# Two evacuation edits in an attention and two-layer feed-forward kernel on one core: who copies the first layer's sums, and where the second layer's stores stand

## The chip, the core and the metric

One Trainium2 chip, of which one core is used. Its engines each work through their own queue in order: PE (TensorE) multiplies and writes into PSUM, ACT (ScalarE) and DVE (VectorE) read PSUM and do element-wise work, SP (SyncE) issues all the DMA transfers of this kernel. The metric is the device time of one execution in microseconds (us); the time before is the median of three runs.

## The reference

Attention in chunks, then two feed-forward layers over the 3072 tokens of 512 features (`B*S` by `H*D`), all in float32:

```
out = _attn_ref(q, k, v, mem_k, mem_v)      # chunks of 32 queries, 64 keys each: 8 memory + 16 left + 32 + 8 right
x   = out.transpose(0, 2, 1, 3).reshape(B * S, H * D)
h   = np.maximum(x @ w_in, 0.0)             # layer 1: 512 -> 2048
x   = h * h @ w_out                         #          2048 -> 512
h   = x @ w_in2                             # layer 2: 512 -> 2048
g   = np.maximum(h, 0.0) + np.log1p(np.exp(-np.abs(h)))
y   = g @ w_out2                            #          2048 -> 512
```

## The kernel before

**Numbers.** Each float32 operand is split into a high and a low half; a product is three matmuls of 128x128 by 128x512 (high by low, low by high, high by high). ACT makes the high half (a cast) and DVE the low half (a subtraction).

**Layer 1** runs over six blocks of 512 tokens, n = 0 to 5, and in each over 16 steps f = 0 to 15. A step is written in `step(n, f)`: 12 matmuls into a PSUM buffer `hp` (`h_mm`, L292 to L294), then on ACT the relu, the square and the high half `gh` (`act1`, L304, L305, L307, through the buffer `r`), on DVE the low half `gl` (`act1_low`, L313), which is written down one step later, and 12 matmuls that add into the four PSUM accumulators `acc` of the block (`out_mm`, L328). These 12 lag by two steps (`LOOK = 2`), so that the last one of block n is issued behind the `hp` matmuls of step 0 of block n+1, and the first one of block n+1 behind those of its step 2. Between the steps stand the attention of the next block (scores L156, softmax on DVE and ACT L176 to L188, the transposes of the probabilities on DVE L202 in two batches of eight, the values L237) and the preparation of layer 2's weights (loads `cf<-w` L379, then L384 on ACT and L388 to L392 on DVE, split and stored). In all this part the order of every engine is the written one (`manual_schedule()`).

When the sums of a block are complete, `evac` (L333) copies the four accumulators to SBUF, two on ACT (L339) and two on DVE (L337) in turn, and stores each to DRAM (L340). The SBUF tile comes from `tmp`, a tag with three buffers, which the relu's `r` uses as well. A buffer that is handed out again waits until its last reader is done; for `ev` that is the store.

The attention's result of the next block is gathered in the tile `xf` (`p_out`, L253, tag `xf`, one buffer), written at steps 3, 7, 11 and 14, and read at step 15 by `x_split` (L267, L268), which makes layer 1's operands. In the last block `x_load` (L486) uses the same tag for layer 2's input.

**Layer 2** runs over three groups of two blocks. `first_stage` has eight chunks p of 42 matmuls (36 in the first) into PSUM banks (`product`, L745), in which seven products replace eight; ACT copies partial sums to `h` (L775, L777, L784, L765), DVE adds (L786, L792, L794), and `softplus` (L751 to L757: three operations on ACT, four on DVE, in the buffers `cf`) follows. `second_stage` has 16 steps f of 24 matmuls (L833) into all eight PSUM banks, and `g_split` (L404, L399) makes the halves for it. When the 16 steps are done, the eight banks are copied, four on ACT into `cf` (L843) and four on DVE into `tmp` (L840), and stored (L845). Weights are reloaded by `fetch` (L375) in six places, one load as a place comes free; the last `fetch` of a group stands at f = 15. In layer 2 only PE's order is the written one. That of ACT, DVE and SP is set by the scheduler that compiles the kernel, from its own estimate of when things are ready.

Of the kernel before, what the change touches and what calls it, by code (L numbers as in the profile page):

```python
# [10 lines left out]
F32 = mybir.dt.float32  # L11
# [9 lines left out]
P = 128  # L21
# [7 lines left out]
KD = DM // P  # L29
KF = DFF // P  # L30
# [3 lines left out]
BLK = 512  # L34
# [8 lines left out]
NCF = 3  # L43
# [12 lines left out]
def body(ctx: ExitStack, tc: tile.TileContext, qk, vW, w1, w2, out):  # L56
    nc = tc.nc
# [3 lines left out]
    xpool = ctx.enter_context(tc.tile_pool(name="xpool", bufs=1))  # L61
# [6 lines left out]
    x2s = [dram.tile([P, KD, BLK], F32, name=f"x2s{i}") for i in range(NB)]  # L68
# [12 lines left out]
    def cf_tile(k=None, shape=(P, 2, DM), dtype=F32):  # L81
        if k is None:
            k = cf_at[0] = (cf_at[0] + 1) % NCF
        return sb.tile(list(shape), dtype, tag=f"cf{k}", name="cf", bufs=1)
# [230 lines left out]
    acc = [None] * 4  # L315
# [15 lines left out]
                )  # L331

    def evac(blk):  # L333
        for m in range(4):
            e = tmp("ev")
            if m % 2:
                nc.vector.tensor_copy(e, acc[m])  # L337
            else:
                nc.scalar.copy(out=e, in_=acc[m])  # L339
            nc.sync.dma_start(out=x2s[blk][:, m, :], in_=e)  # L340


    at_ctx = tc.tile_pool(name="at", bufs=1)
# [5 lines left out]
    def tmp(name):  # L349
        return sb.tile([P, BLK], F32, tag="tmp", name=name, bufs=3)  # L350
# [11 lines left out]
    def out_step():  # L362
        n, f, g, cols = pending.pop(0)
        out_mm(f, g, cols)
        if f == KF - 1:
            evac(n)
# [119 lines left out]
    def x_load(grp, k):  # L486
        t = xpool.tile([P, 2, 2, BLK], F32, tag="xf", name="x2f")
        for i in range(2):
            nc.sync.dma_start(out=t[:, :, i], in_=x2s[2 * grp + i][:, k::2])
        xf_t[2, grp, k] = t  # L490

    def x_jobs(grp, k):
        d = {}

        def sums(i):
            b11, b12, b21, b22 = (xf_t[2, grp, k][:, j // 2, j % 2] for j in range(4))
            if i == 0:
                if grp == 0:
                    t = late[0].tile([P, 4, BLK], F32, tag="r2", name="xs")
                    d["t"] = t[:, 0], t[:, 1], t[:, 2]  # L500
                else:
                    d["t"] = [tmp("xs") for _ in range(3)]
            t3, t2, t4 = d["t"]
            if i == 0:
                todo = (t3, b22, b12), (b12, b12, b11)
            else:
                todo = (t2, b22, b12), (t4, b21, t2)
            for o, a, b in todo:
                nc.vector.tensor_tensor(out=o, in0=a, in1=b, op=ALU.subtract)
            d["x"] = b11, b12, t2, b22, b21, t3, t4  # L510

        def split(i):
            if k == 0:
                xo[grp, i] = wpool.tile([P, 2, 2, BLK], F32R, tag=f"w{i}", name=f"xo{i}")
            t = xo[grp, i]
            halves(t[:, 0, k], t[:, 1, k], d["x"][i], late=(grp == 0))

        return [lambda: sums(0), lambda: sums(1)] + [lambda i=i: split(i) for i in range(7)]


    with tc.manual_schedule(engines={mybir.EngineType.SP}):
# [198 lines left out]
        def fetch():  # L720
            i = at_load[0]
            if i == len(loads):
                return
            at_load[0] += 1
            key, src = loads[i]
            pool, tag = places[i % len(places)]
            t = pool[0].tile(list(src.shape), F32R, tag=tag, name="ws")
            store(t, src)
            ws[key] = t

        def bank():
            i = at_bank[0] = (at_bank[0] + 1) % 8
            if i < 4:
                return (ps, pl[0])[i % 2].tile([P, BLK], F32, tag="ps", name="bk")
            return pa.tile([P, DM], F32, tag=f"acc{i - 4}", name="bk")
# [12 lines left out]
        def softplus(p, i):  # L748
            h = ht[p][:, i]
            z, l, c = (cf_tile(k) for k in range(3))  # L750
            nc.scalar.activation(out=z, in_=h, func=AF.Abs)  # L751
            nc.scalar.activation(out=z, in_=z, func=AF.Exp, scale=-1.0)
            nc.scalar.activation(out=l, in_=z, func=AF.Ln, bias=1.0)
            nc.vector.tensor_scalar(out=c, in0=z, scalar1=1.0, scalar2=-1.0, op0=ALU.add, op1=ALU.add)
            nc.vector.tensor_tensor(out=c, in0=z, in1=c, op=ALU.subtract)  # L755
            nc.vector.scalar_tensor_tensor(out=h, in0=h, scalar=0.0, in1=l, op0=ALU.max, op1=ALU.add)
            nc.vector.tensor_tensor(out=h, in0=h, in1=c, op=ALU.add)  # L757

        def g_split(f, t):
            g = gs[f, t] = g_tiles()  # L760
            halves(*g, ht[f // 2][:, f % 2, t])

        def last_product(grp, p, a):
            product(grp, 6, ws.pop((grp, "b", p))[:, 1], a, False)
            nc.scalar.copy(out=ht[p][:, 1, 0], in_=a)  # L765
            fetch()
# [35 lines left out]
        def second_stage(grp, prev):  # L802
            banks = {}
            if grp + 1 < NGR:
                todo = {f: [] for f in range(KF)}
                for k in range(2):
                    j = x_jobs(grp + 1, k)
                    for f, n in zip((3, 4, 5, 6, 7) if k == 0 else (9, 10, 11, 12, 13), (2, 2, 2, 2, 1)):
                        todo[f] += j[:n]
                        j = j[n:]  # L810
            for f in range(KF):
                w = ws[grp, "o", f // 2][:, f % 2]
                if grp + 1 < NGR and f in (1, 8):
                    x_load(grp + 1, f // 8)
                if f + 1 < KF:
                    for t in range(2):
                        g_split(f + 1, t)
                for i in SOFT_B.get(f, ()):
                    softplus(i // 2, i % 2)
                if grp + 1 < NGR:  # L820
                    for job in todo[f]:
                        job()
                for t in range(2):
                    gh, gl = gs.pop((f, t))
                    for m in range(4):
                        if f == 0:
                            banks[t, m] = bank()
                            if (t, m) == (0, 3):
                                last_product(grp, *prev)
                        bk = banks[t, m]  # L830
                        s = slice(m * P, (m + 1) * P)
                        for j, (a, b) in enumerate(((gh[:, s], w[:, 1]), (gh[:, s], w[:, 0]), (gl[:, s], w[:, 0]))):
                            nc.tensor.matmul(out=bk, lhsT=a, rhs=b, start=(f == 0 and j == 0), stop=(f == KF - 1 and j == 2))  # L833
                if f % 2:
                    fetch()
            for t in range(2):
                for m in range(4):
                    if m % 2:
                        e = tmp("ev")
                        nc.vector.tensor_copy(e, banks[t, m])  # L840
                    else:
                        e = cf_tile((2 * t + m // 2) % NCF)[:, 0]
                        nc.scalar.copy(out=e, in_=banks[t, m])  # L843
                    r = (2 * grp + t) * BLK + m * P
                    nc.sync.dma_start(out=out[r:r + P, :], in_=e)  # L845

        xq = {}
        for k in range(2):
# [17 lines left out]
        with tc.manual_schedule(engines={mybir.EngineType.PE}):  # L866
            for grp in range(NGR):
                second_stage(grp, first_stage(grp))
# [45 lines left out]
```

## Time and profile before

| | us |
|---|---|
| median of 3 runs (1121.87 to 1123.51) | 1122.61 |
| the profiled execution | 1124.83 |
| its span in the trace | 1123.1 |
| PE busy | 1088.1 (97%) |
| DVE busy | 761.0 (68%) |
| ACT busy | 589.8 (53%) |
| mean granted TensorE clock | 0.988 of full speed |

Rows of a timeline read: start in us from the span's start, duration, engine, line, operation, output from inputs, shapes, count, and in brackets the idle time of that engine just before, with what ended it. "<-DVE gl L313" means that the wait was ended by DVE's instruction of line 313 that wrote `gl`. A matmul row lasts longer than the distance to the next one, since matmuls overlap; the distance is what counts.

### The profile page before, as it was taken

The numbers are of one execution on the slowest core, as the hardware profiler recorded it, in microseconds if no ns is written. First come the engines' busy times: TensorE is split into PE (matmuls) and PEld (weight loads), VectorE is DVE, ScalarE is ACT, GpSimd is POOL, SyncE is SP. The second block draws the span as 40 slices with busy tenths as digits, with TensorE's granted clock in tenths as the row PEclk, the third lists the DMA queues.
The fourth block names the chain that finished last, engine by engine and source line by source line (L and its number), as shares of the span: only waits on it lengthen the run. The fifth ranks groups of instructions, "written<-read, shape, count | busy, mean of one in ns | idle before, by whom it ended". The sixth has DMA issues, their size and how long they took to land.

```text
span 1123.1 us, 18576 instructions
## 1 busy us (share of the span) xinstructions
PE 1088.1 (97%) x7592; PEld 893.1 (80%) x7592; DVE 761.0 (68%) x1239; ACT 589.8 (53%) x914; POOL 0.7 (0%) x6
## 2 busy tenths in 40 slices
PE   5899999999999999999999999999999999999998
PEld 4668878878887887788888878888788888788887
DVE  6899576667667666785533499953598963699822
ACT  3567544444554445454544577642577642676622
POOL 0000000000000000000000000000000000000000
PEclk9899999999999999999999999999999999999999
DMA  9941244445335544343440755422655441755202
GB/s 365 379 186 54 63 138 144 147 156 175 102 118 173 175 147 164 132 168 132 149 142 1 265 192 208 170 103 103 207 197 215 150 141 66 244 191 221 76 1 75
DMA packets 49428, 174.99 MB, mean 156 GB/s; under 512 B 5312, under 2 KB 5312, under 8 KB 41152
## 3 DMA queue, kind: packets, MB, share of 16 engines
q1 hardware_dynamic: 49344, 173.82, 44.2%
q8 instruction: 59, 0.97, 0.3%
q14 instruction: 25, 0.20, 0.1%
HBM read 138.15 MB, written 35.65 MB: 155 GB/s over the span
## 4 chain that ended last, share of the span: by engine, by line
PE 88%; DVE 6%; DMA 2%; ACT 2%; issue 1%; SPq 0%; DVEq 0%; ACTq 0%
PE bk L833 23%; PE acc L328 22%; PE bk L745 18%; PE hp L292 7%; PE hp L293 7%; PE hp L294 7%; PE xs L237 1%; DMA out<-cf 1%; DVE pt L202 1%; PE xs L156 1%; DMA x2s<-ev 1%; DVE cf L110 1%; DVE cf L107 1%; PE sc L156 1%; PE xp L237 1%
## 5 line engine op out<-in xcount | busy, mean ns | idle before, releaser
L328 PE MATMUL acc<-gh,w 128*128 128x512 f32 (+1 forms) x776 | 243.1, 395 | 0.9 <-DVE w L122 0.9
L833 PE MATMUL bk<-ws,gh 128*128 128x512 f32 x768 | 236.5, 389 | 0.0
L745 PE MATMUL bk<-xo,ws 128*128 128x512 f32 x1008 | 230.8, 390 | 2.3 <-ACT h L784 1.5
L745 PEld LDWEIGHTS bk<-xo,ws 128*128 128x128 f32 x1008 | 188.9, 188 | 43.0 <-ACT h L784 2.3
L328 PEld LDWEIGHTS acc<-gh,w 128*128 128x128 f32 x776 | 146.8, 191 | 31.8 <-DVE w L122 1.3
L833 PEld LDWEIGHTS bk<-ws,gh 128*128 128x128 f32 x768 | 144.1, 188 | 30.2
L328 PE MATMUL acc<-gl,w 128*128 128x512 f32 (+1 forms) x388 | 153.5, 396 | 11.7 <-DVE gl L313 11.7
L292 PE MATMUL hp<-xh,w 128*128 128x512 f32 (+1 forms) x388 | 154.8, 399 | 3.5 <-ACT pt L218 3.1
L293 PE MATMUL hp<-xl,w 128*128 128x512 f32 (+1 forms) x388 | 152.7, 393 | 0.0
L294 PE MATMUL hp<-xh,w 128*128 128x512 f32 (+1 forms) x388 | 152.0, 392 | 0.0
L833 PE MATMUL bk<-ws,gl 128*128 128x512 f32 x384 | 149.4, 389 | 0.0
L399 DVE TENSOR_TENSOR gl<-h,gh 128x512 fp32r<-128x512 f32 x96 | 66.1, 690 | 84.3 <-ACT gh L404 84.0
L404 ACT CAST gh<-h 128x512 fp32r<-128x512 f32 x96 | 59.4, 622 | 112.2 <-PE bk L833 111.9
L304 ACT ACTIVATE r<-hp 128x512 f32<-128x512 f32 (+1 forms) x97 | 57.2, 590 | 110.5 <-PE hp L294 96.6
L313 DVE TENSOR_TENSOR gl<-r,gh 128x512 fp32r<-128x512 f32 (+1 forms) x97 | 66.3, 683 | 67.2 <-ACT gh L307 66.7
L328 PEld LDWEIGHTS acc<-gl,w 128*128 128x128 f32 x388 | 74.2, 191 | 29.8 <-DVE gl L313 14.5
L292 PEld LDWEIGHTS hp<-xh,w 128*128 128x128 f32 x388 | 74.6, 192 | 19.8 <-ACT pt L218 3.3
L294 PEld LDWEIGHTS hp<-xh,w 128*128 128x128 f32 x388 | 74.7, 193 | 15.4
L293 PEld LDWEIGHTS hp<-xl,w 128*128 128x128 f32 x388 | 74.6, 192 | 14.7 <-DVE xl L282 0.2
L833 PEld LDWEIGHTS bk<-ws,gl 128*128 128x128 f32 x384 | 72.1, 188 | 14.7
L202 DVE STREAM_TRANSPOSE pt<-t 32x128 f32<-32x128 f32 x256 | 77.5, 303 | 4.3
L751 ACT ACTIVATE cf<-h 128x1024 f32<-128x1024 f32 x48 | 51.0, 1062 | 27.8 <-DVE cf L755 19.9
(82 smaller groups left out, 1143.6 us busy)
## 6 DMA issues: line engine op xcount, KB each, us to landing
ws<-wa SPq DMA_DIRECT2D x24, 1024.0 KB, 4.9
ws<-wo SPq DMA_DIRECT2D x24, 1024.0 KB, 4.8
ws<-wb SPq DMA_DIRECT2D x24, 768.0 KB, 4.4
r<-w SPq DMA_DIRECT2D x16, 1024.0 KB, 10.6
cf<-w SPq DMA_DIRECT2D x32, 512.0 KB, 5.1
qk<-qk SPq DMA_DIRECT2D x46, 336.0 KB, 4.9
v<-vW SPq DMA_DIRECT2D x44, 256.0 KB, 4.9
wo<-cf SPq DMA_DIRECT2D x16, 512.0 KB, 2.9
```

What stands on the lines that cost most here:

```text
L202: nc.vector.transpose(pt[b:b + 32, g], t[g * 32:(g + 1) * 32, i, h])
L292: nc.tensor.matmul(out=hp, lhsT=b, rhs=xh[:, c], start=(c == 0), stop=False)
L293: nc.tensor.matmul(out=hp, lhsT=a, rhs=xl[:, c], start=False, stop=False)
L294: nc.tensor.matmul(out=hp, lhsT=a, rhs=xh[:, c], start=False, stop=(c == KD - 1))
L304: nc.scalar.activation(out=r, in_=hp, func=AF.Relu)
L313: nc.vector.tensor_tensor(out=gl, in0=r, in1=gh.bitcast(F32), op=ALU.subtract)
L328: nc.tensor.matmul(out=acc[m][:, cols], lhsT=a, rhs=b, start=(f == 0 and j == 0 and cols.start == 0), stop=(f == KF - 1 and j == 2),)
L399: nc.vector.tensor_tensor(out=lo, in0=x, in1=hi.bitcast(F32), op=ALU.subtract)
L404: nc.scalar.copy(out=hi, in_=x)
L745: nc.tensor.matmul(out=bk, lhsT=a, rhs=b, start=(start and n == 0), stop=(n == 5), skip_group_check=not start)
L751: nc.scalar.activation(out=z, in_=h, func=AF.Abs)
L833: nc.tensor.matmul(out=bk, lhsT=a, rhs=b, start=(f == 0 and j == 0), stop=(f == KF - 1 and j == 2))
```

## The change

`evac` takes one tile of the tag `xf` for all four accumulators, copies all four on ACT, and stores each part from it. The `tmp` buffers and DVE have no part in it any more. In `second_stage` the copies and stores of a bank stand right behind the last matmul that adds into it, inside the loop over f, m and t, and so ahead of the `fetch` of f = 15; before, they came in a loop of their own behind it.

```
     def evac(blk):
+        e = xpool.tile([P, KD, BLK], F32, tag="xf", name="ev")
         for m in range(4):
-            e = tmp("ev")
-            if m % 2:
-                nc.vector.tensor_copy(e, acc[m])
-            else:
-                nc.scalar.copy(out=e, in_=acc[m])
-            nc.sync.dma_start(out=x2s[blk][:, m, :], in_=e)
+            nc.scalar.copy(out=e[:, m], in_=acc[m])
+            nc.sync.dma_start(out=x2s[blk][:, m, :], in_=e[:, m])
...
                             nc.tensor.matmul(out=bk, lhsT=a, rhs=b, start=(f == 0 and j == 0), stop=(f == KF - 1 and j == 2))
+                        if f == KF - 1:
+                            if m % 2:
+                                e = tmp("ev")
+                                nc.vector.tensor_copy(e, bk)
+                            else:
+                                e = cf_tile((2 * t + m // 2) % NCF)[:, 0]
+                                nc.scalar.copy(out=e, in_=bk)
+                            r = (2 * grp + t) * BLK + m * P
+                            nc.sync.dma_start(out=out[r:r + P, :], in_=e)
                 if f % 2:
                     fetch()
-            for t in range(2):
-                for m in range(4):
-                    if m % 2:
-                        e = tmp("ev")
-                        nc.vector.tensor_copy(e, banks[t, m])
-                    else:
-                        e = cf_tile((2 * t + m // 2) % NCF)[:, 0]
-                        nc.scalar.copy(out=e, in_=banks[t, m])
-                    r = (2 * grp + t) * BLK + m * P
-                    nc.sync.dma_start(out=out[r:r + P, :], in_=e)
```

PE's order is the same in both kernels. In the changed kernel lines from `evac` on carry a number that is 3 lower, and 6 lower behind `second_stage`'s loop.

**DVE at the first block boundary.** `pt` are the attention's transposed probabilities, `ev` the evacuated sums, `gl` the low half that PE's next `acc` matmuls read. Before:

```order
158 L202 STREAM_TRANSPOSE pt<-t 32x128 x8
159 L337 COPY ev<-acc_696 128x512
160 L337 COPY ev<-acc_698 128x512
161 L313 TENSOR_TENSOR gl<-r,gh 128x512
162 L202 STREAM_TRANSPOSE pt<-t 32x128 x8
```

Now:

```order
157 L188 TENSOR_TENSOR t<-t,s 128x512
158 L202 STREAM_TRANSPOSE pt<-t 32x128 x8
159 L313 TENSOR_TENSOR gl<-r,gh 128x512
160 L202 STREAM_TRANSPOSE pt<-t 32x128 x8
161 L385 TENSOR_SCALAR cf<-cf 128x512
```

`gl` follows the transposes at once; the two copies are gone. Every later evacuation loses its two in the same way.

**ACT at the same boundary.** `t` is the softmax's exponential, `cf` a weight load's first step, `r` the next step's relu. Before:

```order
120 L178 ACTIVATE t<-t 128x512
121 L339 COPY ev<-acc_695 128x512
122 L339 COPY ev<-acc_697 128x512
123 L384 ACTIVATE cf<-cf 128x512
124 L304 ACTIVATE r<-hp 128x512
```

Now:

```order
120 L178 ACTIVATE t<-t 128x512
121 L336 COPY ev<-acc_695 128x512
122 L336 COPY ev<-acc_696 128x512
123 L336 COPY ev<-acc_697 128x512
124 L336 COPY ev<-acc_698 128x512
125 L381 ACTIVATE cf<-cf 128x512
126 L304 ACTIVATE r<-hp 128x512
```

Two copies more stand ahead of L384 (now L381) and the relu.

**DVE from the end of the first group into the second group of layer 2**, where the scheduler orders it. `ev<-bk` are the eight banks' copies, `h<-bk,h` the additions L792, L786, L794 of one chunk after the other, the rest is `softplus` and, as `gl`, `g_split`. Before:

```order
675 L840 COPY ev<-bk 128x512 x3
676 L792 TENSOR_TENSOR h<-bk,h 128x512
677 L840 COPY ev<-bk 128x512
678 L786 TENSOR_TENSOR h<-bk,h 128x512
679 L794 TENSOR_TENSOR h<-bk,h 128x512
680 L754 TENSOR_SCALAR cf<-cf 128x1024
681 L755 TENSOR_TENSOR cf<-cf 128x1024
682 L756 SCALAR_TENSOR_TENSOR h<-h,cf 128x1024
683 L757 TENSOR_TENSOR h<-h,cf 128x1024
684 L786 TENSOR_TENSOR h<-bk,h 128x512
685 L792 TENSOR_TENSOR h<-bk,h 128x512
686 L754 TENSOR_SCALAR cf<-cf 128x1024
```

Now:

```order
665 L783 TENSOR_TENSOR h<-bk,h 128x512
666 L791 TENSOR_TENSOR h<-bk,h 128x512
667 L751 TENSOR_SCALAR cf<-cf 128x1024
668 L752 TENSOR_TENSOR cf<-cf 128x1024
669 L753 SCALAR_TENSOR_TENSOR h<-h,cf 128x1024
670 L754 TENSOR_TENSOR h<-h,cf 128x1024
671 L783 TENSOR_TENSOR h<-bk,h 128x512
672 L751 TENSOR_SCALAR cf<-cf 128x1024
673 L396 TENSOR_TENSOR gl<-h,gh 128x512
674 L789 TENSOR_TENSOR h<-bk,h 128x512
675 L752 TENSOR_TENSOR cf<-cf 128x1024
676 L396 TENSOR_TENSOR gl<-h,gh 128x512
```

All four copies now come ahead of the additions (row 663, left out), and from the second L786 (now L783) on the additions, `softplus` and `g_split` stand in another order. It is the order that the first group has in both kernels, on DVE as on ACT, from its first addition to its last bank, and the third group has it too up to where the second group prepares the next input.

**SP at the end of the first group** held `ws<-wb` ahead of the eight stores `out<-cf`, `out<-ev`; now the eight stores stand ahead of it. The same holds at the end of the second group. In the third, which has nothing to reload, nothing moves.

## Rows read from the trace of the kernel before

**Rows 1.** Waits of PE: engine, line, ended by; us in total, times, longest.

```profile
PE acc L328 <- DVE gl L313: 11.7, 7, 2.4
PE bk L745 <- ACT h L784: 1.5, 2, 0.8
PE bk L745 <- DVE h L794: 0.9, 2, 0.7
```

**Rows 2.** Timeline of the first block boundary, all engines: start, us, what, idle.

```profile
143.97 0.57 ACT L339 COPY ev<-acc 128x512 f32<-128x512 f32 x1
...
144.56 8.25 SPq L340 DMA_DIRECT2D x2s<-ev  x4
...
148.52 0.69 DVE L337 COPY ev<-acc 128x512 f32<-128x512 f32 x1
...
150.18 0.61 PE L328 MATMUL acc<-gh,w 128*128 128x512 f32 x2
151.77 0.69 DVE L337 COPY ev<-acc 128x512 f32<-128x512 f32 x1 [2.55 <-DMA x2s<-ev]
152.49 0.69 DVE L313 TENSOR_TENSOR gl<-r,gh 128x512 fp32r<-128x512 f32 x1
...
153.24 0.50 PE L328 MATMUL acc<-gl,w 128*128 128x512 f32 x1 [2.45 <-DVE gl L313]
...
157.66 0.69 DVE L313 TENSOR_TENSOR gl<-r,gh 128x512 fp32r<-128x512 f32 x1
...
157.92 0.40 PE L292 MATMUL hp<-xh,w 128*128 128x512 f32 x1
```

**Rows 3.** Timeline of the first chunks of the first group of layer 2.

```profile
627.22 19.20 PE L745 MATMUL bk<-xo,ws 128*128 128x512 f32 x84
...
646.37 0.69 DVE L794 TENSOR_TENSOR h<-bk,h 128x512 f32<-128x512 f32 x1
...
647.11 5.05 PE L745 MATMUL bk<-xo,ws 128*128 128x512 f32 x21 [0.69 <-DVE h L794]
```

**Rows 4.** Stretches: us, busy PE PEld DVE ACT POOL, PEclk, DMA share, GB/s.

```profile
153.00:158.00 5.00, 4.76 (x14) 3.78 (x15) 4.70 (x13) 2.54 (x5) 0.00 (x0) 0.66 0.55 157
...
353.00:356.00 3.00, 3.00 (x14) 2.44 (x14) 2.78 (x10) 1.74 (x3) 0.00 (x0) 1.00 0.75 237
```

**Rows 5.** Timeline of PE at the second, third and fourth boundary.

```profile
250.15 0.61 PE L328 MATMUL acc<-gh,w 128*128 128x512 f32 x2
...
257.05 0.40 PE L292 MATMUL hp<-xh,w 128*128 128x512 f32 x1
...
349.99 0.61 PE L328 MATMUL acc<-gh,w 128*128 128x512 f32 x2
...
355.14 0.39 PE L292 MATMUL hp<-xh,w 128*128 128x512 f32 x1
...
448.04 0.61 PE L328 MATMUL acc<-gh,w 128*128 128x512 f32 x2
...
455.07 0.40 PE L292 MATMUL hp<-xh,w 128*128 128x512 f32 x1
```

**Rows 6.** DMA issues: transfer, queue, count, KB each, median us to landing.

```profile
x2s<-ev SPq DMA_DIRECT2D x24, 256.0 KB, 2.8
...
out<-cf SPq DMA_DIRECT2D x12, 256.0 KB, 4.5
```

**Rows 7.** Timeline where layer 2's groups meet, first to second, then second to third.

```profile
790.52 6.96 PE L745 MATMUL bk<-xo,ws 128*128 128x512 f32 x30
790.72 0.32 SPq L375 DMA_DIRECT2D ws<-wb  x1
...
797.08 0.58 ACT L843 COPY cf<-bk 128x512 f32<-128x512 f32 x1 [3.05 <-DMA out<-cf]
...
798.21 4.15 PE L745 MATMUL bk<-xo,ws 128*128 128x512 f32 x17 [0.72 <-ACT h L784]
...
962.46 21.83 PE L745 MATMUL bk<-xo,ws 128*128 128x512 f32 x95 [0.76 <-ACT h L784]
```

## The prediction

> **What bounds the kernel now.** I read the page first: PE is busy for 97% of the span, so the end is set by PE's work plus the pauses in it, and an edit on ACT, DVE or SP counts only where it takes away or adds a pause of PE. Second the list of PE's waits: nearly all that is left is PE waiting for `gl`, 11.7 us in seven times; in layer 2 only 1.5 us behind ACT's L784 and 0.9 us behind DVE's L794 [rows 1]. Third the timeline around the places where these waits lie.
>
> At the first block boundary the reader is to see one chain [rows 2]. ACT's first copy of `acc` runs at 143.97, but SP's four stores spread over 8.25 us from 144.56, because the copies come late. DVE reaches its first copy at 148.52, behind eight transposes. Its second copy starts only at 151.77, after 2.55 us of waiting for a store of `ev` to land: four `ev` tiles share three buffers with the relu's `r`. Behind that copy in DVE's queue stands `gl` at 152.49, and PE, which needs it, goes on at 153.24 after 2.45 us. So it isn't the copying that PE waits for, nor the accumulators; it is a subtraction that sits in a queue behind a buffer.
>
> What the boundary costs is more than the wait. Undisturbed matmuls follow each other at (19.20 - 0.39) / 83 = 0.2266 us [rows 3]. At the first boundary PE starts `acc` at 150.18 and, 15 matmuls later, the last three of the next `hp` among them, stands at 157.92: 7.74 us instead of 3.40, a loss of 4.34 us. The wait is part of that; the rest is a slower clock, granted at 0.66 on the mean from 153 to 158 [rows 4], a mixture of the two levels of 1.2 and 2.4 GHz, after an idle PE. The second to fourth boundary, each over 12 matmuls (2.72 us undisturbed) [rows 5]: 257.05 - 250.15 = 6.90, loss 4.18; 355.14 - 349.99 = 5.15, loss 2.43; 455.07 - 448.04 = 7.03, loss 4.31. At the third the clock stayed at 1.00 [rows 4], and so the loss is the pause alone. Sum of four: **15.26 us**. The fifth boundary has no softmax in front of `gl`, and PE waits for nothing there; the sixth evacuation, into layer 2, holds no PE wait either.
>
> **The change part by part.** *Evacuation on ACT alone, from a tile of its own.* It takes 2 copies of 0.69 us off DVE at each of six places and adds 2 of 0.57 us to ACT. At the first boundary `gl` then starts where DVE's first copy started, at 148.52, and ends by 148.52 + 0.69 = 149.21. PE uses it in the third matmul of `acc`, due at 150.18 + 2 x 0.2266 = 150.63 [rows 2], 1.4 us later. At the other boundaries PE and DVE stand in the same pattern. So the wait goes as a whole, and with no pause I expect the clock to stay up. Value taken: all 15.26 us. The other bound is that nothing of it goes, if something else holds `gl`.
>
> What is late next? Three candidates, each bounded by the same rows. ACT: four copies in a row, from 143.97 at 0.57 us each, end by 146.3, and the first accumulator is needed again at 150.18, so they have 3.9 us to spare. Behind them in ACT's queue stand L384 and the next relu; the relu's input is complete 12 matmuls before 150.18, at 147.5, so the copies don't delay it. L384 needs a weight load, and would now be reached some 2.5 us sooner than behind the late copies, so a wait for that load is what I can't exclude; until 3.9 us are used up it costs nothing. DVE: the second `gl` came 157.66 - 152.49 = 5.17 us after the first; from 148.52 on that gives 153.69, end 154.4, and PE wants it at 150.18 + 24 x 0.2266 + 0.45 = 156.1. SP: the four stores go out one behind the other, about 2.8 us to landing [rows 6], and the loads behind them leave 6 us sooner.
>
> The new tile has one buffer, `xf`. Its former content was read by `x_split` one step earlier, ahead of the softmax in the same queues, so the first copy finds it free. It is written again by `p_out` three steps on, 72 matmuls or 16 us later, when the stores (2.8 us) have long landed. Cost nothing; the cover is those 16 us.
>
> Here a rule of the Trainium skill speaks against the change: "TensorEngine Tiling (Array Packing)", section "PSUM Bottleneck", says to use both ScalarE and VectorE for PSUM evacuation. By that rule one engine would lengthen the evacuation; the sum with it is the third rival's. The trace of before shows the two engines held by the buffer and not by their speed.
>
> *Stores ahead of the last reload.* Before, SP held `ws<-wb` until PE had left the last step (790.72), and the eight stores behind it; the fourth `cf` copy waited 3.05 us for the first of them to land, L784 stood behind that copy, and PE waited 0.72 us for L784 [rows 7]. PE's product should have gone on at 790.52 + 30 x 0.2266 = 797.32 and did at 798.21: 0.89 us. The second place has 0.76 us of wait in place of 0.72, so 0.93 us. Now the first store leaves as its copy ends: the first bank is complete 21 matmuls before 790.52, at 785.8, its copy by 786.4, the store lands 4.5 us later (the median [rows 6]) at 790.9, and the fourth copy is done by 791.5; L784 is due only 24 matmuls behind 790.52, at 796.0. Gain 1.82 us. The displaced reload leaves some 2 us later and is the third chunk's, 78 matmuls or 17 us on: nothing.
>
> *The order of layer 2's second and third group* is new, though the edit doesn't touch them. It is now the order of the first group, so the first group's trace prices it: L794 at 646.37 comes late in DVE's queue, and PE, due at 627.22 + 84 x 0.2266 = 646.26, goes on at 647.11, a loss of 0.85 us [rows 3]; the remaining 0.2 us of that wait in [rows 1] falls on the last chunk. Cost 2 x (0.85 + 0.2) = 2.1 us, since before these two groups had no such wait. Bounds: 0, if DVE is ahead there, to twice that. I take 2.1, as the DVE chain that leads to L794 begins at an addition that PE itself releases. So layer 2 as a whole loses 0.3 us.
>
> *The tail* is unchanged: the last group reloads nothing, and its copies already followed each bank.
>
> Sum: -15.26 - 1.82 + 2.1 = **-15.0 us**. The profiled execution took 1124.83 us, 2.22 more than the median; 1124.83 - 15.0 = 1109.8, less 2.2 is **1107.6 us**.
>
> **The rivals.**
> *Layer 2 pauses not at all.* The earlier stores let `softplus` begin sooner and L794's wait doesn't return. For it: before, these groups had none. Against: the order is the first group's. 1122.61 - 15.26 - 1.82 = 1105.5 us.
>
> *ScalarE alone becomes the boundary's limit.* Its copies, then L384 waiting for a load, make relu and `gl` late, and PE pauses elsewhere. If the two copies more lie on the path in full at the five boundaries, 5 x 2 x 0.57 = 5.7 us, time 1113.3 us. This is what the skill's rule named above would make of it. Against: the spare 3.9 us.
>
> *The change doesn't free `gl`.* The wait for a store moves from `tmp` to `xf` and PE pauses as before: 1122.6 us. Against: 16 us between two uses of that buffer.
>
> *Slower.* DVE's new order in groups two and three makes PE pause at each of the 7 later chunks of both, with the slow clock behind each as at the first boundary: 0.85 + (4.34 - 2.43) = 2.76 us, 14 times, 38.6 us; 1122.61 - 17.08 + 38.6 = 1144 us. It decides for slower from 17.08 / 14 = 1.2 us a chunk. Against: in the first group, with this order, one chunk of seven paused by 0.85 us.
>
> **How the numbers follow.** Forecast 0.72 (1107.6, by itself 1106 to 1110), no pause in layer 2 0.10, ScalarE's limit 0.12, `gl` not freed 0.03, slower 0.03. The range takes in the first three: 1104.8, a little under the second, for the scatter of about 1 us between runs, to 1113.5. That leaves 0.06 and some of the tails outside. A measurement of this kernel can tell 0.2%, 2.2 us, from no change. Faster by more than that: the first three, 0.94. Within 0.2%: 0.03. Slower: 0.03.
>
> **What would show it.** In the profile after, the PE wait for `gl` of L313 should fall from 11.7 to about 2.4 us, four of its seven times gone, and the clock at the boundaries should read 1.00. `x2s<-ev` should be issued four in 2 us and not over 8. Of layer 2, PE's wait for L784 should be gone, and that for L794 should be three times the 0.9 us of before. The forecast is wrong if PE waits at the boundaries for ACT (an `acc` or `hp` buffer), if the slow clock stays without a pause, or if L794 holds PE in more than one or two chunks of a group.

## The result, and the profile after

The changed kernel takes 1108.13 us (median of four runs, 1106.41 to 1110.64), the kernel before beside it 1122.24 us. The ratio is 0.9879 with a 95% interval of 0.9853 to 0.9905, so 14.1 us (1.2%) are gone. The forecast was 1107.6 us.

The first view is the list of PE's waits of the changed kernel (engine, line, ended by; us, times, longest), the answer to [rows 1].

```profile
PE bk L742 <- DVE h L791: 2.5, 6, 0.7
...
PE acc L328 <- DVE gl L313: 2.2, 2, 1.8
```

The wait for `gl` fell from 11.7 us in seven to 2.2 us in two, of which one of 1.8 us stands near the start, where nothing was changed. The wait for ACT's L784 is no longer in the list, and that for L794 (now L791) is there six times instead of twice.

The second view is the timeline of the first block boundary of the changed kernel, the answer to [rows 2].

```profile
139.91 2.03 ACT L336 COPY ev<-acc 128x512 f32<-128x512 f32 x4
...
140.50 2.32 SPq L337 DMA_DIRECT2D x2s<-ev  x4
...
141.81 0.69 ACT L381 ACTIVATE cf<-cf 128x512 f32<-128x512 f32 x1
...
144.44 0.69 DVE L313 TENSOR_TENSOR gl<-r,gh 128x512 fp32r<-128x512 f32 x1
...
146.11 0.61 PE L328 MATMUL acc<-gh,w 128*128 128x512 f32 x2
146.56 0.39 PE L328 MATMUL acc<-gl,w 128*128 128x512 f32 x1
...
148.83 0.39 PE L292 MATMUL hp<-xh,w 128*128 128x512 f32 x1
```

The four copies run one behind the other and the four stores leave within 2.32 us instead of 8.25. `gl` ends at 145.13, 1.43 us ahead of the matmul that reads it (146.56), and PE passes from `acc` (146.11) to the next `hp` (148.83) in 2.72 us, the 12 matmuls' own time. Before, the same 12 took 6.90, 5.15 and 7.03 us at the second to fourth boundary [rows 5].

The third view compares stretches: start, layer 1 and layer 2, cut where PE enters the last run of 24 `acc` matmuls (two steps in a row) ahead of the first and of the sixth evacuation (columns as in [rows 4]; the third number from the end is the granted clock). First the kernel before, then the changed one.

```profile
0.00:132.76 132.76, 113.38 (x1429) 91.73 (x1429) 105.75 (x155) 77.05 (x121) 0.70 (x6) 0.94 0.58 219
132.76:617.87 485.11, 475.81 (x3970) 389.77 (x3970) 311.61 (x664) 233.23 (x412) 0.00 (x0) 0.99 0.41 137
```

```profile
0.00:128.71 128.71, 110.69 (x1429) 89.38 (x1429) 105.64 (x155) 77.10 (x121) 0.70 (x6) 0.97 0.59 226
128.71:598.48 469.77, 469.77 (x3969) 386.55 (x3970) 304.78 (x654) 237.63 (x422) 0.00 (x0) 1.00 0.42 142
```

Layer 1 lost 485.11 - 469.77 = 15.34 us, and PE is busy in the whole of it. The start is 4.05 us shorter, with the same instructions on every engine; in the runs below it takes between 128.5 and 133.3 us whatever is changed, so it is scatter, and the profiled execution was the fastest of the four. The start's granted clock differs between the two executions too, 0.94 and 0.97 in the rows. Layer 2, from 617.87 and 598.48 to the last matmul, takes 501.3 us before and 502.3 after: 1 us longer.

The fourth view is the timeline where layer 2's first and second group meet in the changed kernel, the answer to [rows 7].

```profile
770.74 0.59 ACT L837 COPY cf<-bk 128x512 f32<-128x512 f32 x1 [0.82 <-PE bk L830]
771.18 20.56 PE L742 MATMUL bk<-xo,ws 128*128 128x512 f32 x90
...
772.52 0.40 SPq L372 DMA_DIRECT2D ws<-wb  x1
...
791.69 0.68 DVE L791 TENSOR_TENSOR h<-bk,h 128x512 f32<-128x512 f32 x1
...
792.43 7.82 PE L742 MATMUL bk<-xo,ws 128*128 128x512 f32 x33 [0.68 <-DVE h L791]
```

The fourth copy waits for PE alone, no store any more, and PE runs through 90 matmuls instead of stopping after 30. It then stops for DVE's L791, at the very place and for the very time that the first group shows in [rows 3].

### The profile page after: what moved, and what is told of

The parts are those of the page before. It is cut to its first block, busy times and chain, and to the rows that moved or that the text cites. A ratio compares the mean times of both kernels' runs of the same rounds, so it can differ in the third digit from the quotient of the medians.

```text
span 1104.6 us, 18583 instructions
## 1 busy us (share of the span) xinstructions
PE 1080.2 (98%) x7592; PEld 887.1 (80%) x7592; DVE 753.2 (68%) x1227; ACT 595.4 (54%) x926; POOL 0.7 (0%) x6
## 4 chain that ended last, share of the span: by engine, by line
PE 91%; DVE 5%; ACT 2%; issue 1%; DMA 0%; SPq 0%; DVEq 0%
PE bk L830 23%; PE acc L328 23%; PE bk L742 18%; PE hp L292 8%; PE hp L293 7%; PE hp L294 7%; PE xs L237 1%; PE xs L156 1%; DVE cf L110 1%; DVE cf L107 1%; PE sc L156 1%; PE xp L237 1%; DVE h L753 1%; PE xpe L237 1%; ACT w L118 1%
## 5 line engine op out<-in xcount | busy, mean ns | idle before, releaser
L328 PE MATMUL acc<-gh,w 128*128 128x512 f32 (+1 forms) x776 | 238.9, 389 | 0.4 <-DVE w L122 0.4
L328 PEld LDWEIGHTS acc<-gh,w 128*128 128x128 f32 x776 | 144.0, 188 | 30.5 <-DVE w L122 0.8
L328 PE MATMUL acc<-gl,w 128*128 128x512 f32 (+1 forms) x388 | 150.5, 388 | 2.2 <-DVE gl L313 2.2
L294 PEld LDWEIGHTS hp<-xh,w 128*128 128x128 f32 x388 | 73.8, 190 | 15.3
```

Of the source, the lines that this page charges most:

```text
L294: nc.tensor.matmul(out=hp, lhsT=a, rhs=xh[:, c], start=False, stop=(c == KD - 1))
L328: nc.tensor.matmul(out=acc[m][:, cols], lhsT=a, rhs=b, start=(f == 0 and j == 0 and cols.start == 0), stop=(f == KF - 1 and j == 2),)
```

## The experiments

**One half of the change at a time.** The first run has `evac` of the change and layer 2's stores of before.

```
+        e = xpool.tile([P, KD, BLK], F32, tag="xf", name="ev")
         for m in range(4):
-            ... tmp, copy on DVE or ACT, store
+            nc.scalar.copy(out=e[:, m], in_=acc[m])
+            nc.sync.dma_start(out=x2s[blk][:, m, :], in_=e[:, m])
```

> Only the first half of the change: all four accumulators are copied on ACT into the xf tile; the stores of layer 2 stay in their own loop behind the last reload. Theory (the whole gain comes from the four block boundaries, layer 2 is a wash): 15.3 us faster than before, about 1107; PE's wait for gl (L313) down from 11.7 to about 2.2 us; PE's wait for ACT's L784 stays at 1.5 us and that for DVE's L794 at 0.9 us. Rival (the stores ahead of the reload carry a part of the gain): under 12 us faster.

Measured: 1108.2 us beside 1121.56 us of before, ratio 0.9873 (0.9850 to 0.9897). PE's waits in this kernel (L781 is L784 of before, L791 is L794):

```profile
PE acc L328 <- DVE gl L313: 2.4, 3, 1.8
...
PE bk L742 <- ACT h L781: 1.2, 2, 0.6
PE bk L742 <- DVE h L791: 0.8, 2, 0.7
```

This half has the gain: layer 1 takes within 0.1 us what it takes in the changed kernel, and the two waits of layer 2 are there as before (1.5 and 0.9 us). The rival asked for less than 12 us, and the interval, 11.6 to 16.8 us, just reaches it; what decides against it is the next run.

The second run has `evac` of before and the new place of layer 2's stores.

```
+                        if f == KF - 1:
+                            ... copy bank (t, m), store it
                 if f % 2:
                     fetch()
-            for t in range(2): for m in range(4): ... copy, store
```

> Only the second half: copies and stores of layer 2's banks behind each bank's last matmul, ahead of the last reload; evac as before. Theory: -1.8 us for L784's wait, +2.1 us for L794's wait in groups two and three: within 1 us of before (1121 to 1123); PE's wait for L784 gone, for L794 about 2.5 us in six times; the gl wait of 11.7 us stays. Rival (earlier stores help in themselves): 1.8 us or more faster, 1120 or less, with no new L794 wait.

Measured: 1123.22 us (12 runs) beside 1121.56 us, ratio 1.0013 (0.9997 to 1.0028). PE's waits:

```profile
PE acc L328 <- DVE gl L313: 11.8, 7, 2.5
...
PE bk L745 <- DVE h L794: 2.7, 6, 0.8
```

This half gains nothing; at 1.7 us slower its interval still reaches just below 1. The traces show a small cost: from the cut ahead of the sixth evacuation to the last matmul, layer 2 takes 502.3 to 502.5 us in the five traces with the new place of the stores (the changed kernel twice, this run and the two with reductions below) and 501.0 to 501.3 us in the four with the old place (before, the run above and the two that follow). So the second half of the change loses 1 us or a little more. The wait for L784 is gone and that for L794 came, with the order of DVE and ACT in groups two and three that the change has: the new order belongs to the stores and not to `evac`.

**Which part of `evac` does it.** The change frees `gl` in two ways at once: no copy of DVE stands in front of it, and no copy waits for a store. The next run has the tile of its own but both engines.

```
+        e = xpool.tile([P, KD, BLK], F32, tag="xf", name="ev")
         for m in range(4):
-            e = tmp("ev")
             if m % 2:
-                nc.vector.tensor_copy(e, acc[m])
+                nc.vector.tensor_copy(e[:, m], acc[m])
             else:
-                nc.scalar.copy(out=e, in_=acc[m])
-            nc.sync.dma_start(out=x2s[blk][:, m, :], in_=e)
+                nc.scalar.copy(out=e[:, m], in_=acc[m])
+            nc.sync.dma_start(out=x2s[blk][:, m, :], in_=e[:, m])
```

> The xf tile as in the change, but copies on ACT and DVE in turn as before; stores of layer 2 as before. Theory (the wait for a store of ev is what holds gl): DVE does its two copies in a row behind the transposes, gl ends some 1.4 us later than in the changed kernel and just in time (spare 1.4 us minus 1.4 us), so 13 to 15.3 us faster than before, 1107 to 1109, with pauses of PE under 0.3 us at a boundary. Rival (it is DVE's two copies in front of gl, whatever they wait for): half of the gain or less, 1114 or more.

Measured: 1107.54 us, ratio 0.9878 (0.9854 to 0.9902). The timeline of its first boundary:

```profile
149.04 1.29 DVE L337 COPY ev<-acc 128x512 f32<-128x512 f32 x2
...
150.36 0.69 DVE L313 TENSOR_TENSOR gl<-r,gh 128x512 fp32r<-128x512 f32 x1
150.69 0.61 PE L328 MATMUL acc<-gh,w 128*128 128x512 f32 x2
...
151.14 0.46 PE L328 MATMUL acc<-gl,w 128*128 128x512 f32 x1
```

Two copies in a row, no wait between them, `gl` ends at 151.05, and PE reads it on time at 151.14. So DVE's two copies in front of `gl` use up the spare time almost exactly: the 12 matmuls of the four boundaries take 0.1, 0.3, 0.1 and 0.1 us more than their 2.72. The wait for a store between the copies was what could not be afforded.

The other way round: ACT alone, but with the three buffers of before.

```
         for m in range(4):
             e = tmp("ev")
-            if m % 2:
-                nc.vector.tensor_copy(e, acc[m])
-            else:
-                nc.scalar.copy(out=e, in_=acc[m])
+            nc.scalar.copy(out=e, in_=acc[m])
             nc.sync.dma_start(out=x2s[blk][:, m, :], in_=e)
```

> All four copies on ACT, but from tmp with its three buffers as before; stores of layer 2 as before. Theory (gl is held only through DVE's queue): ACT's third and fourth copy and the relu behind them now wait for stores of ev to land, some 8 us in all, but gl on DVE is free, and PE needs that relu's gl only 5.4 us later than the first one: 13 to 15.3 us faster than before, 1107 to 1109. Rival (a boundary without a buffer of its own pauses PE in any case, now through ACT, by a late relu): less than half of the gain, 1115 or more, with PE waiting for hp buffers or for the second gl.

Measured: 1107.5 us, ratio 0.9873 (0.9847 to 0.9898). The timeline of its first boundary:

```profile
141.77 1.06 ACT L336 COPY ev<-acc 128x512 f32<-128x512 f32 x2
...
142.36 5.28 SPq L337 DMA_DIRECT2D x2s<-ev  x4
...
146.12 1.17 ACT L336 COPY ev<-acc 128x512 f32<-128x512 f32 x2 [3.30 <-DMA x2s<-ev]
146.30 0.69 DVE L313 TENSOR_TENSOR gl<-r,gh 128x512 fp32r<-128x512 f32 x1
...
148.42 0.39 PE L328 MATMUL acc<-gl,w 128*128 128x512 f32 x1
```

ACT still waits 3.30 us for a store, but `gl` on DVE runs at 146.30, and PE reads it at 148.42 without a pause. Either part of the edit of `evac` is enough by itself, as far as the intervals can tell; what cost the time was the conjunction, a wait for a store in the queue that also holds `gl`.

**The spare time and the price of a pause.** Two kernels put reductions on DVE in front of `gl` at the first four boundaries of the changed kernel (4 or 6 of 0.69 us; their line numbers are one higher).

```
+    pad = const.tile([P, 1], F32, name="pad")
...
+        if blk < NB - 2:
+            for _ in range(4):
+                nc.vector.tensor_reduce(out=pad, in_=e[:, 0], axis=AX.X, op=ALU.max)
```

> The changed kernel with four extra reductions of about 0.7 us on DVE between the transposes and gl at the first four boundaries (they read the evacuated tile, their result is not used). It measures the spare time and the price of a pause. Theory: gl ended 1.4 us before PE wanted it, so 2.8 us more make a pause of about 1.4 us at each of four boundaries, 5.8 us in all, and a pause that short leaves the clock up: 5 to 7 us slower than the changed kernel, about 1114. Rival (no spare time at all, any delay shows in full): 11 us or more, 1119.

> The same with six reductions, 4.2 us. Theory: pauses of about 2.8 us at four boundaries, 11.4 us in all, and behind some of them the slow clock as in the kernel before, 1.8 us each: 11 to 18 us slower than the changed kernel, 1119 to 1126, near the kernel before. Rival (the slow clock before had nothing to do with the pause): 11.4 us and granted clock 1.00 at all four boundaries.

Measured: with four 1115.5 us (ratio to before 0.9955, 0.9940 to 0.9969), some 6 to 8 us above the changed kernel; with six 1126.71 us (1.005, 1.0032 to 1.0068), some 17 to 19 us above it. In the traces layer 1, between the same cuts as above, takes 476.64 and 488.46 us instead of the 469.77 of the changed kernel, 6.9 and 18.7 more. The first rows are DVE's and PE's at the first boundary with four, then PE's with six reductions, and the granted clock behind the four boundaries with six (columns as in [rows 4]).

```profile
148.58 2.85 DVE L341 TENSOR_REDUCE pad<-ev 128x1 f32<-128x512 f32 x4
...
152.08 0.50 PE L329 MATMUL acc<-gl,w 128*128 128x512 f32 x1 [1.24 <-DVE gl L314]
```

```profile
153.07 0.50 PE L329 MATMUL acc<-gl,w 128*128 128x512 f32 x1 [2.68 <-DVE gl L314]
...
153.00:158.00 5.00, 4.93 (x15) 3.89 (x16) 4.70 (x13) 1.06 (x2) 0.00 (x0) 0.66 0.00 0
253.00:258.00 5.00, 4.55 (x11) 3.58 (x12) 4.72 (x13) 2.39 (x4) 0.00 (x0) 0.50 0.00 0
354.00:359.00 5.00, 4.06 (x11) 3.20 (x12) 4.72 (x13) 2.40 (x4) 0.00 (x0) 0.66 0.01 3
455.00:460.00 5.00, 4.86 (x21) 4.04 (x22) 4.70 (x13) 0.34 (x1) 0.00 (x0) 1.00 0.00 0
```

2.85 us of reductions give a pause of 1.24 us by the row, 1.40 us by the distance between starts (the difference of the two counts is explained below): the 1.4 us to spare are there. With six, the pauses of 2.67 to 2.87 us are followed by a slow clock at three of four boundaries; at the fourth, after the same 2.67 us, it stayed at 1.00. With four it stayed at 1.00 everywhere.

**A version that is faster than both.** What is left in layer 2 is PE waiting for L791 ahead of the last product of the chunk before. This kernel issues that product one product later.

```
-                if prev is not None:
-                    last_product(grp, *prev)
-                else:
+                if prev is None:
                     b = bank()
                     product(grp, 4, wb_t[:, 0], b, True)
                 product(grp, 2, wa_t[:, 2], a, False)
                 nc.scalar.copy(out=h[:, 0, 1], in_=a)
+                if prev is not None:
+                    last_product(grp, *prev)
```

> The changed kernel with the last product of the chunk before issued on PE one product later (behind product 2 of the chunk instead of ahead of it), which gives DVE's L794 (here L791) 6 x 0.2266 = 1.36 us more. Theory (PE's remaining pauses in layer 2 are L794 being late in DVE's queue by 0.7 us): they go, 3 groups x (0.85 + 0.4): 2.5 to 4 us faster than the changed kernel, about 1105. Rival (another order of DVE and ACT follows and another operation is late): no gain, with a wait of PE for another line in layer 2.

> Evacuation on ACT alone as in the change, stores of layer 2 in their old place behind the reload, and the last product one product later as in the run before. Theory: the pause for L794 in the first group goes (0.85 + 0.4 us), that for L784 behind the late stores stays (0.9 us twice): within 1.5 us of the changed kernel, 1106 to 1108. Rival (the old place of the stores is better, as it keeps another order in groups two and three): faster than the run before by 1 us or more.

Measured: with the whole change 1103.43 us, ratio to before 0.9848 (0.9830 to 0.9866); with `evac` alone 1106.33 us, 0.9870 (0.9853 to 0.9887). Two more runs put the changed kernel and this version on one chip.

> The changed kernel once more, beside the next run on one chip, to tell the two apart. Theory: 14 to 15 us faster than before.

> The changed kernel with the last product one product later, once more. Theory (layer 2 without PE pauses, 3.8 us shorter in the trace): 3 to 5 us faster than the changed kernel beside it. Rival (the difference of the first runs was the scatter of the start-up): within 1 us of it.

Measured: 1109.74 us (0.9885, 0.9868 to 0.9902) and 1103.84 us (0.9840, 0.9827 to 0.9853). The intervals no longer touch: the later product gains some 5 us on the change, 18 us on the kernel before. The chain of waits of the faster kernel, from the last `acc` matmuls to the first of the last stretch, shows why (start, us, what):

```profile
607.74 73.57 PE bk L742 x324
681.31 2.05 PE bk L830 x9
683.36 1.39 PE bk L742 x6
684.75 85.06 PE bk L830 x375
769.81 74.93 PE bk L742 x330
```

The chain runs through PE alone; no wait of PE for L791 is left. From the same cut to the last matmul layer 2 takes 498.5 us instead of 502.3. With the stores in their old place the same edit leaves the pause for the late copy (1.0 us in two waits), and layer 2 takes 500.4 us. So by the traces the new place pays 1.9 us once L791 is no longer late; the intervals of the two runs' times overlap. Why the runs differ by a little more than the 3.8 us of the traces stays open; the start's scatter would cover it (131.9 and 129.7 us in the traces of the last two runs).

## Why the prediction was right

The sum was -15.0 us, measured 14.1, and the terms can be checked one by one.

The boundaries: forecast 15.26 us, found 15.34 in the traces. Both are read from the same execution of the kernel before, so what the agreement shows is that nothing of this loss was left. Every step held: DVE's `gl` starts where its first copy started, the clock stays at 1.00 behind the boundaries, ACT's four copies end long before `acc` is needed. The spare 1.4 us of `gl` were measured as 1.43, and the run with four reductions charged a delay only beyond them.

The rule of "TensorEngine Tiling (Array Packing)", section "PSUM Bottleneck", in the Trainium skill, to use both ScalarE and VectorE for PSUM evacuation, made no difference here: with a free buffer, ACT alone took 1108.2 us and both engines 1107.54 us, and their intervals overlap. The section gives the rule for matmuls that tiling has sped up, where the PSUM copy may become the bottleneck; here the copying isn't what PE waits for.

The stores: forecast -1.82 us, and the wait for L784 went as the step says, the fourth copy now waiting for PE alone.

The new order in groups two and three: forecast +2.1 us; if the stores gave their 1.8 us in full, layer 2's balance (1.0 + 1.8) leaves 2.8 for it. The pause itself repeats to a hundredth of a microsecond, since the order is the first group's and the chain to it starts at an addition that PE releases: due at 771.18 + 90 x 0.2266 = 791.57, PE went on at 792.43, 0.86 us. The term that was mis-sized is the last chunk's, for which I took the 0.2 us of idle time:

```profile
848.81 0.39 PE L830 MATMUL bk<-ws,gl 128*128 128x512 f32 x1
849.36 1.66 PE L742 MATMUL bk<-xo,ws 128*128 128x512 f32 x6 [0.16 <-DVE h L791]
```

The idle time counts from the modelled end of a matmul, 0.39 us behind its start, while the next one would have started after 0.2266. So a pause costs its idle time and 0.16 us more: 849.36 - 848.81 - 0.2266 = 0.32. For the large pause I had taken the distance between starts, and for this small one I should have too. The six matmuls behind it took 0.12 us longer than their like in the faster version (1.54 us there). Together a group loses 0.86 + 0.32 + 0.12 = 1.30 us, where the sum has 1.05; that makes 2.6 of the 2.8 us.

Of the rivals, layer 2 without pauses (1105.5) and ScalarE's limit (1113.3) were both in the range and both wrong: L791 holds PE six times, and PE's 12 matmuls take 2.72 us at all four boundaries. (ScalarE's limit is the second rival of the list; the sentence on the rule calls it the third.) What I named as uncertain, L384 (now L381) reached sooner and waiting for its load, holds nothing up that PE needs: at the first boundary it ran at 141.81, right behind the copies, and the next one, which waited 2.93 us for its load and ran at 148.44, cost PE nothing.

The slow clock was right in the sum and less certain than the text has it. In the run with the stores alone, the boundaries have the pauses of before (2.13 to 2.46 us) and the clock fell behind one of them, not three. The rows are PE's from `acc` to the next `hp` at the first, second and fourth boundary, then the clock behind all four:

```profile
147.74 0.61 PE L328 MATMUL acc<-gh,w 128*128 128x512 f32 x2
...
153.24 0.39 PE L292 MATMUL hp<-xh,w 128*128 128x512 f32 x1
...
246.14 0.61 PE L328 MATMUL acc<-gh,w 128*128 128x512 f32 x2
...
251.49 0.39 PE L292 MATMUL hp<-xh,w 128*128 128x512 f32 x1
...
444.04 0.61 PE L328 MATMUL acc<-gh,w 128*128 128x512 f32 x2
...
449.47 0.39 PE L292 MATMUL hp<-xh,w 128*128 128x512 f32 x1
...
150.00:155.00 5.00, 4.18 (x18) 3.47 (x19) 4.67 (x13) 2.17 (x4) 0.00 (x0) 1.00 0.58 157
249.00:254.00 5.00, 4.93 (x22) 4.06 (x23) 4.72 (x13) 3.00 (x5) 0.00 (x0) 1.00 0.51 157
347.00:352.00 5.00, 4.87 (x14) 3.88 (x15) 4.72 (x13) 3.07 (x6) 0.00 (x0) 0.66 0.49 159
447.00:452.00 5.00, 4.93 (x22) 4.09 (x23) 4.70 (x13) 1.78 (x4) 0.00 (x0) 1.00 0.14 54
```

Beyond the 2.72 us of the 12 matmuls these three lose 2.78, 2.63 and 2.71 us with the clock up, where the kernel before lost 4.34, 4.18 and 4.31 with the slow clock; its third boundary lost 2.43 with the clock up. So about 10.5 us of the 15.3 belong to the pauses, and the other 4.8 to the clock, 1.6 us for each of three falls. Layer 1 takes 481.9 us there and 485.1 in the trace of before. Which pauses the slow clock follows changes from one execution to the next, and my sum stands on one execution that had three slow boundaries of four: against the execution with one, the same edit would be worth 481.9 - 469.8 = 12.1 us. That the sum came out as near as it did is in this part luck.

## What to carry to other kernels

Where PE waits for an operation, look at what stands in front of it in its engine's queue and what that waits for: here a copy that waited for a store to land held a subtraction that had nothing to do with either, and taking the copy off the queue or giving it a free buffer was equally good within the scatter of the runs. Count a pause by the distance between starts, with the slow clock that may follow, and not by its idle time. When an edit makes a scheduler order later code anew, look whether the new order already stands somewhere in the old trace: it prices itself, pauses included.

## What the runs showed of the hardware that I had not expected

The same pause of TensorE isn't always followed by the slow clock. Over three executions with four such boundaries each (the kernel before, the stores alone, six reductions), pauses of 2.1 to 2.9 us were followed by a granted clock under 1.00 seven times and by 1.00 five times, with a fall after 2.13 us and none after 2.46 and 2.67 us; the four of 1.2 to 1.4 us in the run with four reductions were followed by none. Where the same boundary can be compared with and without it, a fall cost about 1.6 us.
